# One-core linear attention and mixture of experts: 64-token transposes, keyed state first, deeper load buffers, routing one step at a time, zeros after the attention

## Chip, cores and metric

The kernel runs on one core of a Trainium2 chip. The metric is the device time of one execution in microseconds (us). The kernel before took 589.33 us, the median of three runs (588.52, 589.33 and 590.4).

## What is computed

A linear attention with a decaying state (4 batches, 8 heads, 768 tokens, 48 features a head), whose output, seen as 3072 tokens of 384 features, goes into a mixture of 8 experts with noisy top-2 routing. Everything is float32.

```python
for t in range(S):                                   # S = 768
    cur = einsum('bhd,bhe->bhde', u * k[t], v[t])
    y[:, :, t] = einsum('bhd,bhde->bhe', r[t], state + cur)
    state = w[:, :, None] * state + einsum('bhd,bhe->bhde', k[t], v[t])
x = y.transpose(0, 2, 1, 3).reshape(3072, 384)
noisy = x @ w_gate + log1p(exp(x @ w_noise)) * noise
top2 = the two largest of noisy, top2_w = their softmax
for e in range(8):
    out[mask] += top2_w * (relu(x[mask] @ w1[e]) @ w2[e])   # 384 -> 1024 -> 384
```

## The kernel before, in words

The kernel has two stages. The **attention** goes over 24 blocks of 128 tokens: iteration i takes chunk i // 4 of batch i % 4, so that chunk 0 (iterations 0 to 3) has no state yet and chunk 5 (20 to 23) leaves none. The **experts** follow, expert 0 in three pieces of its tokens, the others in two; each piece is a first layer (`p1`, L984) and a second (`p2`, L1018), and the result is scattered to `out`.

The order on each engine is the order of the program text (`manual_schedule`); each engine takes its own instructions strictly in that order, and semaphores tie them together. One iteration of the attention is made of:

- loads of k, r and v for block i + 3 (`load`, L139, issued from SyncE, which also writes x and loads weights in the same queue). Four buffers each (`NLD`).
- on GpSimd, `prep_k(i + 2)` (keys by powers of the decay, L349) and `uterm_a(i + 2)` (the u term, L356 and L360), two instructions for each product, and the scaling of the state (L430).
- on TensorE, `trans(i + 1)`: four transposes of 128x128 for k, four for r (L387); `xtrans(i - 1)`: three for the finished x (L475); `kvup` (L417, 16 matmuls for the state); `yout` (L448, 32 matmuls of the masked scores and, from chunk 1, 16 of the state); `logits(i - 1)` (L489, 12 matmuls); `scores(i + 1)` (L399, 16 matmuls of 64 rows, two of which share the array).
- on VectorE, the copy of r out of PSUM with its weights (`rT`, L392), the sum of the u term (`c`, L368), for i up to 8 its product with v (`cv`, L377; after that on ScalarE, L380), the output `x` (L465), the state sum (`zt`, L429), and the two masks of the scores (`am`, L407).
- on ScalarE, the copies of k (L390) and x (L477) out of PSUM, the state's block form (`zblock`, L437), the logits (L491).

Into this order the program lays the **routing**. `route(g)` is a generator of some 55 small VectorE steps for a group of 8 blocks (64 columns wide at most); `rstep(us)` takes as many steps from it as a credit in microseconds allows, in three places of an iteration (0.6, 0.85 and 0.2 us). Most steps read what the step just ahead of them wrote. Routing of blocks 0 to 7 runs from iteration 8, that of 8 to 15 after it, that of 16 to 23 in expert 0. Weights of expert 0 are split into a high and a low part: one ScalarE copy (L313), one VectorE difference (L318) for each of seven pieces (`W_LD`, `W_HI`, `W_LO`). In iteration 21 (`I_EARLY`) the first two tiles of expert 0 are gathered by GpSimd DMAs (`xgather`, L903) and in iteration 22 transposed (`xT`, L926). From iteration 16 on `zero_out` writes half of the zeros that `out` starts from (8 of 16 DMAs), the rest follow in the first layer of expert 0.

Of the kernel before, what the change touches and what calls it, by code (L numbers as in the profile page):

```python
# [31 lines left out]
STEPS_A = 0.6  # L32
STEPS_B = 0.85
STEPS_KV = 0.2
# [5 lines left out]
NLD = 4  # L40
XT_AT = 4
# [5 lines left out]
W_LD = {1: (0,), 3: (1,), 4: (2,), 5: (3,), 6: (4,), 7: (5,), 8: (6,)}  # L47
W_HI = {4: (0,), 5: (1,), 6: (2,), 7: (3,), 8: (4,), 21: (5,), 22: (6,)}
W_LO = {4: (0,), 5: (1,), 6: (2,), 7: (3,), 8: (4,), 22: (5,)}
# [3 lines left out]
def kernel(  # L53
# [44 lines left out]
    psum = ctx.enter_context(tc.tile_pool(name="psum", bufs=1, space=bass.MemoryType.PSUM))  # L98
    dram = ctx.enter_context(tc.tile_pool(name="dram", bufs=1, space=bass.MemoryType.DRAM))
# [7 lines left out]
    att_pool = [att]  # L107

# [18 lines left out]
    rd = [att.tile([128, H, 64], F32, name=f"rd{j}", bufs=1) for j in range(NLD)]  # L127
    rt, kt, vt = {}, {}, {}

    def load(i, part=(0, 3)):  # L130
        c, b = divmod(i, B)
        for nm, src, dst in (("kt", k, kt), ("rt", r, rt), ("vt", v, vt))[part[0]:part[1]]:
            if nm == "rt":
                t = rd[i % NLD][:, :, :D]
            elif i or nm == "vt":
                t = att.tile([128, H, D], F32, name=nm, bufs=NLD)
# [23 lines left out]
    pwarm = psum.tile([128, 512], F32, name="pwarm", tag="kv")  # L160

    def warm(n):
# [4 lines left out]
    warm(WARM0)  # L167
# [14 lines left out]
    mneg = const.tile([128, 1, 128], I32, name="mneg")  # L182
# [17 lines left out]
    kT, rT = {}, {}  # L200

    def turn0(src, dst, pw, nm):
        pt = psum.tile([128, NP, 128], F32, name="pt0", tag="pa", bufs=2)
        for p in range(NP):
            nc.tensor.transpose(pt[:, p, :], src[:, 2 * p:2 * p + 2, :].rearrange("p a b -> p (a b)"), ident)
        t = att.tile([128, NP, 128], F32, name=nm, bufs=1 if nm == "kT" else 2)
        nc.vector.tensor_mul(t, pt, pw)
        dst[0] = t

    tabk = att.tile([128, H, 64], F32, name="tabk", bufs=1)  # L210
    turn0(kd[0], kT, pwk, "kT")
    ptab = psum.tile([128, NP, 128], F32, name="ptab", tag="pt", bufs=2)
# [3 lines left out]
    turn0(rd[0], rT, pwr, "rT")  # L216
# [7 lines left out]
    nc.vector.tensor_mul(w128, tmpw[:, :, 63:64], tmpw[:, :, 63:64])  # L224
# [4 lines left out]
    kvp = pwarm[:, :NP * D].rearrange("p (a d) -> p a d", d=D)  # L229
# [24 lines left out]
    zrow = att.tile([128, DM], F32, name="zrow", bufs=1)  # L254

    def consts_a():
        nc.vector.tensor_scalar(ltri, idif, 0.0, None, op0=ALU.is_gt)
        nc.gpsimd.memset(ones_b, 1.0)
        nc.gpsimd.memset(acc, 0.0)
        for t in ZB:  # L260
            nc.gpsimd.memset(t, 0.0)
# [3 lines left out]
        nc.vector.tensor_copy(ieu, ie)  # L265
        nc.vector.tensor_scalar(ie_n[:, 0, :], ie, float(LS), None, op0=ALU.mult)
# [7 lines left out]
        nc.gpsimd.iota(thi, pattern=[[1, NT], [0, 2]], base=1, channel_multiplier=0, **imp)  # L274

# [21 lines left out]
    def w_split(e):  # L297
# [3 lines left out]
        def unit(mat, c0, c1, src):  # L301
            def f():
# [7 lines left out]
                nc.sync.dma_start(tv, src)  # L310
                for _ in range(NLAG[0]):
                    yield
# [28 lines left out]
    AM, X, CV, PY, PA = {}, {}, {}, {}, {}  # L341

# [23 lines left out]
    def uterm_b(i):  # L366
        c8 = att.tile([128, H, 1], F32, name="c8")
        nc.vector.tensor_reduce(c8, RKU[i], AX.X, ALU.add)  # L368
        C8[i] = c8
        if i <= GROUPS[0][1]:  # L370
            uterm_c(i)

    def uterm_c(i):
        c8 = C8[i]
        cv = att.tile([128, H, D], F32, name="cv")
        if i <= GROUPS[0][1]:
            nc.vector.tensor_mul(cv, vt[i], c8.to_broadcast([128, H, D]))  # L377
        else:
            for h in range(H):
                nc.scalar.activation(cv[:, h, :], vt[i][:, h, :], AF.Copy, scale=c8[:, h, :])  # L380
        CV[i] = cv

    def trans(i):
        for src, store, nm in ((kd[i % 3], kT, "kT"), (rd[i % NLD], rT, "rT")):
            pt = psum.tile([128, NP, 128], F32, name="pt", tag="pt", bufs=2)
            for p in range(NP):
                nc.tensor.transpose(pt[:, p, :], src[:, 2 * p:2 * p + 2, :].rearrange("p a b -> p (a b)"), ident)  # L387
            t = att.tile([128, NP, 128], F32, name=nm, bufs=1 if nm == "kT" else 2)
            if nm == "kT":
                nc.scalar.activation(t, pt, AF.Copy)  # L390
            else:
                nc.vector.tensor_mul(t, pt, pwr)  # L392
            store[i] = t

    def scores(i):
        pa = [psum.tile([128, NP, 128], F32, name="pa", tag="pa", bufs=2) for _ in range(2)]
        for p in range(NP):
            for s in range(2):
                nc.tensor.matmul(pa[s][:, p, :], kT[i][s * 64:(s + 1) * 64, p, :],  # L399
# [3 lines left out]
    def mask(i):  # L403
        pa = PA[i]
        am = att.tile([128, 2, NP, 128], F32, name="am", bufs=1)
        for s in range(2):
            nc.vector.tensor_tensor(am[:, s].bitcast(I32), pa[s].bitcast(I32),  # L407
                                    mneg.to_broadcast([128, NP, 128]), op=ALU.bitwise_and)
# [11 lines left out]
    def zup(i):  # L420
# [3 lines left out]
        if c == 0:  # L424
            for p in range(NP):
                nc.scalar.activation(Z[b][:, p, :], kvp[:, p, :], AF.Copy, scale=w128[:, p, :])
        else:
            src = att.tile([128, NP, D], F32, name="zt", bufs=1)
# [1010 lines left out]
```

## Time and profile before

| | us |
|---|---|
| median of the runs | 589.33 |
| profiled execution | 590.02 |
| its span, first to last instruction | 588.3 |
| attention, first `py` matmul to the last x | 11.1 to 129.6 |
| busy TensorE, VectorE, ScalarE, GpSimd | 575.7, 359.2, 286.1, 276.9 |

In the profile a busy time is the time in which an engine works on at least one instruction. Matmuls are pipelined, so that their starts, not their durations, tell how fast they follow each other; the same holds for VectorE, where an instruction's duration can reach into the next one's. DMA is the mean busy share of 16 DMA engines.

### The profile page before, as it was taken

To read this page: it belongs to the slowest core of one execution; us is meant where nothing else is said; L and a number is where in the kernel's file an instruction comes from. 1 tells how busy PE (TensorE), PEld (TensorE's weight loads), DVE (VectorE), ACT (ScalarE), POOL (GpSimd) and SP (SyncE) were. 2 spreads that over 40 slices of the span, in tenths; PEclk is the share of its full clock that TensorE was granted. 3 is DMA by queue.
4 is the path that set the end of the run, shared out by engine and by line. 5 is a ranking of instruction groups with operands and counts; after the bars stand their busy time and mean duration, and the time that the engine had idled before them with its cause. 6 is when DMAs were issued, how large, how long until landed. Compare 5 with 4: busy or idle time off the path is not lost.

```text
span 588.3 us, 13208 instructions
## 1 busy us (share of the span) xinstructions
PE 575.7 (98%) x5011; PEld 547.6 (93%) x5012; DVE 359.2 (61%) x855; ACT 286.1 (49%) x726; POOL 276.9 (47%) x422
## 2 busy tenths in 40 slices
PE   8999999989999999999999999999999999999995
PEld 5888898979999999999999999999999999999995
DVE  7899998988875734556454554546355546454331
ACT  3656677752363624455445544454544455445220
POOL 8989876811016543336344442534253446423222
PEclk9999999999999999999999999999999999999998
DMA  9999988946315645655565646464745546423211
GB/s 149 215 227 221 208 178 194 219 129 174 111 35 174 212 123 130 186 125 173 111 183 133 176 122 189 104 184 136 165 128 142 171 124 193 119 81 85 67 36 42
DMA packets 143015, 86.42 MB, mean 147 GB/s; under 512 B 118415, under 2 KB 133006, under 8 KB 142944
## 3 DMA queue, kind: packets, MB, share of 16 engines
q1 hardware_dynamic: 132384, 56.67, 40.0%
q0 software_dynamic: 9936, 28.83, 15.8%
q8 instruction: 41, 0.67, 0.5%
q14 instruction: 30, 0.25, 0.1%
q10 hardware_dynamic: 624, 0.00, 0.1%
HBM read 58.83 MB, written 19.76 MB: 134 GB/s over the span
## 4 chain that ended last, share of the span: by engine, by line
PE 87%; DMA 5%; DVE 4%; POOL 2%; issue 1%; ACT 0%; SPq 0%; POOLq 0%; DVEq 0%
PE ph L984 37%; PE pym L1018 34%; PE py L448 3%; DMA kt<-in_k_dram 2%; PE pa L399 2%; PE pym L1011 2%; PE pym L1009 2%; PE pt L387 2%; DMA stg<-in_moe_w_dram 1%; DMA xg<-xd,GR 1%; DVE am L407 1%; PE pwarm L417 1%; PE pl L489 1%; PE ptm L926 1%; PE ptx L475 1%
## 5 line engine op out<-in xcount | busy, mean ns | idle before, releaser
L1018 PE MATMUL pym<-w1h,hb 128*128 128x384 f32 x768 | 200.8, 338 | 0.0
L988 DVE SCALAR_TENSOR_TENSOR hb<-ph,hb 128x384 fp32r<-128x384 f32 (+1 forms) x136 | 72.3, 533 | 111.8 <-ACT ht L986 61.1
L1018 PEld LDWEIGHTS pym<-w1h,hb 128*128 128x128 f32 x768 | 139.6, 188 | 0.3
L984 PE MATMUL ph<-xh,w0h 128*128 128x384 f32 (+3 forms) x408 | 139.8, 343 | 0.0
L984 PE MATMUL ph<-xh,w0l 128*128 128x384 f32 (+3 forms) x408 | 138.8, 341 | 0.0
L984 PE MATMUL ph<-xl,w0h 128*128 128x384 f32 (+3 forms) x408 | 133.6, 341 | 0.0
L1018 PE MATMUL pym<-w1l,hb 128*128 128x384 f32 x384 | 129.8, 338 | 0.0
L986 ACT ACTIVATE hb<-ph 128x384 fp32r<-128x384 f32 (+1 forms) x136 | 64.3, 473 | 107.0 <-PE ph L984 103.8
L1041 POOL DMA_INDIRECT out_dram<-ot,TK x56 | 59.2, 1058 | 98.5 <-DVE ot L1037 45.9
L903 POOL DMA_INDIRECT xg<-xd,GR x56 | 59.4, 1061 | 69.6 <-DVE GR L768 20.4
L984 PEld LDWEIGHTS ph<-xh,w0h 128*128 128x128 f32 x408 | 76.7, 188 | 3.1
L984 PEld LDWEIGHTS ph<-xh,w0l 128*128 128x128 f32 x408 | 76.7, 188 | 2.6
L984 PEld LDWEIGHTS ph<-xl,w0h 128*128 128x128 f32 x408 | 76.1, 188 | 2.7
L912 POOL DMA_INDIRECT pv<-out_dram,GA x49 | 51.9, 1059 | 47.9 <-DMA out_dram<-ot,TK 35.5
L1018 PEld LDWEIGHTS pym<-w1l,hb 128*128 128x128 f32 x384 | 72.1, 188 | 0.1
L959 ACT ACTIVATE xh<-xj 128x384 fp32r<-128x384 f32 (+1 forms) x42 | 21.1, 502 | 43.7 <-DVE xj L957 38.3
L1026 ACT ACTIVATE ot<-pym 128x384 f32<-128x384 f32 x39 | 18.9, 485 | 39.3 <-PE pym L1018 24.0
L448 PE MATMUL py<-vt,am 128*64 128x48 f32 x768 | 36.8, 219 | 0.7 <-DVE am L407 0.7
L960 DVE TENSOR_TENSOR xl<-xj,xh 128x384 fp32r<-128x384 f32 (+1 forms) x42 | 22.3, 532 | 24.7 <-ACT xh L959 17.5
L945 ACT ACTIVATE pl<-xg 128x768 uint16<-128x768 uint16 (+1 forms) x42 | 35.3, 841 | 0.9 <-DMA xd<-pl 0.9
L318 DVE TENSOR_TENSOR w0l<-stg,w0h 128x1024 fp32r<-128x1024 f32 x24 | 29.4, 1241 | 6.8 <-ACT w0h L313 6.8
L448 PEld LDWEIGHTS py<-vt,am 128*64 128x64 f32 x768 | 32.1, 137 | 1.4 <-DVE am L407 1.0
(255 smaller groups left out, 862.3 us busy)
## 6 DMA issues: line engine op xcount, KB each, us to landing
stg<-in_moe_w_dram SPq DMA_DIRECT2D x24, 512.0 KB
stg<-in_moe_w_dram SPq DMA_DIRECT2D x32, 384.0 KB
rd<-in_r_dram SPq DMA_DIRECT2D x24, 192.0 KB
vt<-in_v_dram SPq DMA_DIRECT2D x24, 192.0 KB
xd<-x SPq DMA_DIRECT2D x24, 192.0 KB
out_dram<-zrow SPq DMA_DIRECT2D x16, 288.0 KB
kt<-in_k_dram SPq DMA_DIRECT2D x23, 192.0 KB
xg<-xd,GR POOLq DMA_INDIRECT x56
```

What stands on the lines that cost most here:

```text
L318: nc.vector.tensor_sub(lo, tv, hi.bitcast(F32))
L448: nc.tensor.matmul(o[qs], lhsT[:, qs], rhs, start=first[q], stop=last, skip_group_check=True)
L903: nc.gpsimd.indirect_dma_start(out=xg[:n], out_offset=None, in_=xd[:rows_of(early_)], in_offset=bass.IndirectOffsetOnAxis(ap=GR[:n, e * NJ ...
L912: nc.gpsimd.indirect_dma_start(out=pv[:n], out_offset=None, in_=out, in_offset=bass.IndirectOffsetOnAxis(ap=GA[:n, e * NJ + t:e * NJ + t + ...
L945: nc.scalar.activation(pl[:n], XG[e, t][:n, :DM].bitcast(U16).rearrange("p (d two) -> p two d", two=2), AF.Copy)
L959: nc.scalar.activation(xh, xj, AF.Copy)
L960: nc.vector.tensor_sub(xl, xj, xh.bitcast(F32))
L984: nc.tensor.matmul(ph[:, :w_], a[:, d, fs], x[:, d, :w_], start=(j == 0), stop=(j == len(q) - 1))
L986: nc.scalar.activation(h_[:, f, 0, :], ph[:, a:b], AF.Relu)
L988: nc.vector.scalar_tensor_tensor(h_[:, f, 1, :], ph[:, a:b], 0.0, h_[:, f, 0, :].bitcast(F32), op0=ALU.max, op1=ALU.subtract)
L1018: nc.tensor.matmul(py, hb[:, f, a, hs], x[:, f, :], start=(j == 0), stop=(j == len(q) - 1))
L1041: st = nc.gpsimd.indirect_dma_start(out=out, out_offset=bass.IndirectOffsetOnAxis(ap=TK[:n, q:q + 1], axis=0), in_=ot[:n], in_offset=None, ...
```

## The change

- **Transposes.** k, r and x are transposed in halves of 64 tokens: each 128x128 transpose becomes two with 64 rows of input and 64 columns of output, on the two row halves of the array, written to two PSUM banks (`KX` for k and x, `RV` for r and the state, `PAB` for the scores).
- **Order.** An iteration begins with `kvup` and `yout`, whose state part comes first and which takes the logits of the block before (in the same PSUM bank); then come the transposes of k and r for block i + 2, the scores of i + 1 and the transposes of the x just made. GpSimd's u term is made for i + 1, its state scaling one iteration later. The state of chunk 0 is scaled on VectorE in one instruction, not on ScalarE in four.
- **Loads.** Six buffers for k, r and v; k and r are loaded 6 blocks ahead, v 5. The room comes from the expert activations `hb` and `ht`, which now lie where the attention's tiles were.
- **Routing.** `one_step()` takes one step; there are eight calls in an iteration: two after the state sum, two after the sum of the u term, one each after x, after `rT`, between the two masks and at the end.
- **Expert weights.** The split of each of the seven pieces is cut into two halves, one in each iteration from `W_AT0`; the loads are spread to iteration 14.
- **Zeros.** All 16 DMAs come in the first layer of expert 0. The x tiles of expert 0's first piece are transposed in iteration 23.
- Some constants move: the zeros of the state blocks from GpSimd to ScalarE, three small VectorE ones behind iteration 0.

```diff
-    def trans(i):
-        for src, store, nm in ((kd[i % 3], kT, "kT"), (rd[i % NLD], rT, "rT")):
-            pt = psum.tile([128, NP, 128], F32, name="pt", tag="pt", bufs=2)
-            for p in range(NP):
-                nc.tensor.transpose(pt[:, p, :], src[:, 2 * p:2 * p + 2, :].rearrange("p a b -> p (a b)"), ident)
...
+    def turn_rows(dst, o, src, base=0):
+        for s in range(2):
+            q = slice(base + s * 64, base + (s + 1) * 64)
+            nc.tensor.transpose(dst[:, s, o:o + 64], src[q], ident[q, q])
...
+    def turn_kr(i):
+        if i >= NT:
+            return
+        for src, dst in ((kd[i % 3], KX), (rd[i % NK], RV)):
             for p in range(NP):
+                turn_rows(dst, p * 64, pair(src, p))
+        kT[i] = att.tile([128, NP, 128], F32, name="kT", bufs=2)
+        nc.scalar.activation(by_row(kT[i]), halves_of(KX, 0, NP), AF.Copy)
+        rT[i] = att.tile([128, NP, 128], F32, name="rT", bufs=2)
+        nc.vector.tensor_mul(by_row(rT[i]), halves_of(RV, 0, NP), by_row(pwr))
+        one_step()
...
+        for h in (slice(0, NP // 2), slice(NP // 2, NP)):
+            nc.vector.tensor_tensor(am[:, :, h].bitcast(I32), pa[:, :, h].bitcast(I32),
+                                    mneg[:, None].to_broadcast([128, 2, NP // 2, 128]), op=ALU.bitwise_and)
+            if h.start == 0:
+                one_step()
...
+    def one_step():
+        k = 0
+        while len(route_q) > k and not at_pe[0]:
+            try:
+                c = next(route_q[k])
...
+            if c == "pe":
+                at_pe[0] = 2
+            return
...
     for i in range(NT):
-        if i + NLD - 1 < NT and i + NLD - 1 > 2:
-            load(i + NLD - 1)
-        if i >= NT - 8:
-            zero_out(i - NT + 8)
-        if i + 1 < NT:
-            trans(i + 1)
...
+        products(i)
+        if i + 6 < NT:
+            load(i + 6, (0, 2))
...
+        if i:
+            kvup(i)
         yout(i)
-        xout(i)
...
+        if i + 5 < NT:
+            load(i + 5, (2, 3))
+        zup_v(i)
         if i:
             zblock(i - 1)
-        rstep(STEPS_B)
...
+            uterm_c(i, CV_EARLY, H)
+            logits_out(i - 1)
+            route_when_done(i - 1)
+        tick()
+        one_step()
+        one_step()
+        if i + 1 < NT:
+            uterm_b(i + 1)
+        one_step()
+        one_step()
+        xout(i)
+        one_step()
         if i == NT - 1:
+            xT_first()
+            turn_x(i)
             p1a = p1(0, 0)
+        else:
+            turn_kr(i + 2)
+            uterm_c(i + 1, 0, CV_EARLY)
             scores(i + 1)
+            turn_x(i)
             mask(i + 1)
+            tick()
+            one_step()
...
     for j, _ in enumerate(p1a):
-        zero_out(8 + j)
+        zero_out(2 * j)
+        zero_out(2 * j + 1)
         rstep(STEPS_P1)
+    zero_out(14)
     zero_out(15)
```

## Rows read from the trace of the kernel before

**Rows 1.** Busy time by stage: span, engines with counts, TensorE clock, DMA share, GB/s.

```profile
11.10:49.60 38.50, 37.52 (x755) 33.31 (x751) 35.90 (x63) 21.27 (x57) 34.78 (x56) 1.00 0.97 212
49.60:97.20 47.60, 47.30 (x1004) 43.23 (x1000) 43.90 (x123) 34.62 (x120) 39.52 (x71) 1.00 0.91 200
97.20:129.60 32.40, 29.91 (x579) 26.67 (x574) 28.64 (x90) 22.83 (x80) 17.79 (x31) 1.00 0.72 180
129.60:588.30 458.70, 452.23 (x2630) 439.15 (x2630) 243.36 (x560) 203.24 (x462) 175.30 (x227) 1.00 0.47 134
```

**Rows 2.** The chain that ended last: start us, length us, what.

```profile
57.35 5.32 DMA kt<-in_k_dram
...
120.24 6.07 DMA xg<-xd,GR
...
126.35 0.55 PE ptm L926 x3
...
129.00 0.56 DVE x L465
...
130.22 1.06 PE ph L984 x9
```

**Rows 3.** TensorE's timeline, one iteration: start us, us, engine, line, operation, shape, count.

```profile
70.03 0.56 PE L417 MATMUL pwarm<-vt,kd 128*48 128x48 f32 x16
...
72.20 0.53 PE L489 MATMUL pl<-wg,xT 128*64 128x64 f32 x12
72.67 1.16 PE L399 MATMUL pa<-rT,kT 64*128 64x128 f32 x16
73.76 0.66 PE L387 MATMUL pt<-ident,kd 128*128 128x128 f32 x4
...
74.69 0.49 PE L475 MATMUL ptx<-ident,x 128*128 128x128 f32 x3
75.11 0.39 PE L417 MATMUL pwarm<-vt,kd 128*48 128x48 f32 x8
```

**Rows 4.** Weight loads by line, 65 to 97 us: count, busy us, mean ns, idle.

```profile
L399 PEld LDWEIGHTS pa<-rT,kT 64*128 64x128 f32 x96 | 5.8, 187 | 0.4
...
L489 PEld LDWEIGHTS pl<-wg,xT 128*64 128x64 f32 x78 | 2.9, 138 | 0.0
L387 PEld LDWEIGHTS pt<-ident,rd 128*128 128x128 f32 x24 | 2.8, 141 | 0.0
```

**Rows 5.** VectorE's timeline, where routing steps meet other work.

```profile
58.29 0.21 DVE L512 SCALAR_TENSOR_TENSOR r1r<-RT,r1r 128x64 f32<-128x64 f32 x1
58.54 0.23 DVE L514 TENSOR_SCALAR RT<-r1r 128x64 f32<-128x64 f32 x1
58.81 0.23 DVE L517 SCALAR_TENSOR_TENSOR RT<-RT,r1r 128x64 f32<-128x64 f32 x1
58.95 0.35 DVE L429 TENSOR_TENSOR zt<-pwarm,z 128x192 f32<-128x192 f32 x1
59.21 1.28 DVE L407 TENSOR_TENSOR am<-pa,mneg 128x512 int32<-128x512 int32 x2
60.41 0.22 DVE L517 SCALAR_TENSOR_TENSOR RT<-RT,r1r 128x64 f32<-128x64 f32 x1
60.54 0.68 DVE L392 TENSOR_TENSOR rT<-pt,pwr 128x512 f32<-128x512 f32 x1
```

**Rows 6.** VectorE's groups by line, 11 to 130 us: busy, mean ns, idle before, releasers.

```profile
L407 DVE TENSOR_TENSOR am<-pa,mneg 128x512 int32<-128x512 int32 x46 | 29.4, 680 | 1.9 <-PE pa L399 1.7
...
L465 DVE TENSOR_TENSOR x<-py,cv 128x384 f32<-128x384 f32 x24 | 13.2, 552 | 2.6 <-PE py L448 1.4 <-ACT r_ob L604 0.9
L368 DVE TENSOR_REDUCE c<-rku 128x8 f32<-128x384 f32 x24 | 13.0, 542 | 1.4 <-POOL rku L360 1.4
...
L318 DVE TENSOR_TENSOR w1l<-stg,w1h 128x768 fp32r<-128x768 f32 x3 | 3.1, 1047 | 0.0
...
L928 DVE TENSOR_TENSOR xl<-ptm,xh 128x384 fp32r<-128x384 f32 x2 | 1.1, 558 | 1.2 <-ACT xh L927 1.2
```

More of the change, by code (lines that the diff above doesn't have):

```diff
@@ L40 @@
 NLD = 4
+NV = 6
+NK = 6
 XT_AT = 4
@@ L126 @@
     kd = [att.tile([128, H, 64], F32, name=f"kd{j}", bufs=1) for j in range(3)]
-    rd = [att.tile([128, H, 64], F32, name=f"rd{j}", bufs=1) for j in range(NLD)]
+    rd = [att.tile([128, H, 64], F32, name=f"rd{j}", bufs=1) for j in range(NK)]
     rt, kt, vt = {}, {}, {}
@@ L449, in acc_mm @@
             first[q] = False
+        for p in range(NP if c else 0):
+            for q in range(2):
+                acc_mm(py[:, 2 * p:2 * p + 2, :], rT[i][:, p, :], ZB[b][:, p, :], q, False)
+        if i:
+            logits(i - 1, not c)
         for p in range(NP):
-            if c:
-                for q in range(2):
-                    acc_mm(py[:, 2 * p:2 * p + 2, :], rT[i][:, p, :], ZB[b][:, p, :], q, False)
             for s in range(2):
@@ L467, in xout, with logits, logits_out @@
         nc.sync.dma_start(xd[i * 128:(i + 1) * 128, :DM], x)
-    LG = {}
-    XT = {}
-    def xtrans(i):
-        pt = psum.tile([128, ND, 128], F32, name="ptx", tag="py1")
+    def logits(i, alone):
         for d in range(ND):
-            nc.tensor.transpose(pt[:, d, :], X[i][:, d * 128:(d + 1) * 128], ident)
-        t = att_pool[0].tile([128, ND, 128], F32, name="xT", bufs=1)
-        nc.scalar.activation(t, pt, AF.Copy)
-        XT[i] = t
-    def logits(i):
+            for q in range(2):
+                qs = slice(q * 64, (q + 1) * 64)
+                nc.tensor.matmul(PL[i][qs], XT[i][:, d, qs], wg[:, d, None, :].to_broadcast([128, LREP, 2 * E]),
+                                 start=alone and d == 0, stop=(d == ND - 1), skip_group_check=True)
+    def logits_out(i):
         g = [i >= a for a, _ in GROUPS].count(True) - 1
@@ L1050, with tick @@
     hold = []
+    load(3)
     wun = w_split(0)
+    route_q = []
+    at_pe = [0]
+    credit = [0.0]
+    def tick():
+        for x in late_mm:
+            x[0] -= 1
+            if x[0] == 1:
+                x[2]()
+        while late_mm and late_mm[0][0] <= 0:
+            late_mm.pop(0)[1]()
+            credit[0] -= 0.25
+        at_pe[0] = max(at_pe[0] - 1, 0)
+    def one_step():
[3 more added lines that the diff above has]
+                c = next(route_q[k])
+            except StopIteration:
+                route_q.pop(k)
+                continue
+            if c == "wait" and k == 0 and FILL:
+                k = 1
+                continue
+            if c == "pe":
+                at_pe[0] = 2
+            return
     consts_a()
@@ L1060 @@
     mask(0)
+    load(4)
+    load(5, (0, 2))
     warm(WARM3)
-    route_q = []
-    at_pe = [0]
-    credit = [0.0]
+    turn_kr(1)
+    uterm_b(0)
+    nc.vector.tensor_mul(w128, tmpw[:, :, 63:64], tmpw[:, :, 63:64])
     def rstep(us, lag=2):
@@ L1246 @@
         wstep()
-    att_pool[0] = late[0]
     step, xt = stepper(STEPS_R, 0, 2, (4, 5, 6))
@@ L1386 @@
                 nc.sync.dma_start(X[i], xd[i * 128:(i + 1) * 128, :DM])
-                xtrans(i)
-                logits(i)
+                pt = psm[0].tile([128, ND, 128], F32, name="s_pt", tag="pt", bufs=2)
+                for d in range(ND):
+                    nc.tensor.transpose(pt[:, d, :], X[i][:, d * 128:(d + 1) * 128], ident)
+                XT[i] = slow.tile([128, ND, 128], F32, name="xT", bufs=1)
+                nc.vector.tensor_copy(XT[i], pt)
+                pl_alone(i)
                 for g in range(len(GROUPS)):
```

249 lines of the change are left out of this document (134 added, 115 removed).

## The prediction

> **What bounds the kernel now.** I read the busy times by stage first. In the last stretch, the experts from 129.6 us on, TensorE is busy 452.2 of 458.7 us [rows 1]; what it does there is not touched, so a gain must come from the attention ahead of it, and it reaches the end in full, as the first matmul of the experts (130.22) follows the last x (129.00) at once [rows 2]. In the attention, 11.1 to 129.6 us, two engines are nearly full: TensorE 37.5 + 47.3 + 29.9 = 114.7 and VectorE 35.9 + 43.9 + 28.6 = 108.4 of 118.5 us [rows 1]. Relief for one of them alone therefore gives only what the other leaves. The chain runs mostly over TensorE, with two intrusions by DMAs: arrivals of k (one of 5.32 us) around 48 to 63 us, and the gather that ends at 126.3 and holds up TensorE for the tiles of expert 0 [rows 2]. One undisturbed iteration takes 75.11 - 70.03 = 5.08 us [rows 3].
>
> **Transposes, on TensorE.** By the starts in [rows 3], k and r take 74.69 - 73.76 = 0.93 us for eight transposes, x 0.42 for three with the change to the next shape; together 1.35. They become 22 halves, eleven pairs that can share the array as the scores do. No row shows such a pair. One bound is the pair of logits (72.67 - 72.20 = 0.47 for six pairs, 0.08 each: 64 columns loaded, 64 streamed), the other the pair of scores (1.09 for eight, 0.136 each: 128 loaded, 128 streamed) [rows 3]. Which is nearer is told by the weight loads: a 128-column load of a transpose lasts 141 ns, like the 64-column load of the logits with 138, while the 128-column load of the scores lasts 187 [rows 4]. I take 0.08: 0.86 us an iteration, 0.49 less than now; with 0.136 it is 1.50, 0.15 more. TensorE's iteration then needs 4.6 us (5.2 at the other end). Matmuls for state, outputs, logits and scores are the same in number; only their order differs.
>
> The Trainium skill speaks against this part: "TensorE: Matmul & The Clock Gate", section LDWEIGHTS, has the time of a load depend on its columns and not on its rows, and half a transpose still loads 128 columns. By that rule nothing is saved. The loads of 141 and 187 ns for the same 128 columns [rows 4] show that columns alone don't set it.
>
> **VectorE, what is added and taken away.** Up to the last x:
> - The seventh weight piece is split inside the attention, not behind it: +1.05 [rows 6].
> - The state of chunk 0 moves here from ScalarE, four instructions like `zt`, which takes 59.21 - 58.95 = 0.26 [rows 5]: +1.05.
> - Three constants come after iteration 0: at most 0.25 each by the step rows [rows 5]: +0.75.
> - More routing. The calls in the code: group 0 has 55 steps and starts at the end of iteration 8; one matmul pause in 13 costs it that iteration; it ends in 16. Group 1 starts in 17, pauses in 21 and reaches step 48 by the last x. Before, it stood at about 41 there. Seven more of 0.14: +1.0.
> - The two `xl` of expert 0's first tiles come after the last x: -1.1 [rows 6].
> - Steps one by one. A step followed by the step that reads it takes 0.25 to 0.27 us to the next start (58.29, 58.54, 58.81); followed by other work it takes 0.13 to 0.14 (58.81 to 58.95, 60.41 to 60.54) [rows 5]. So 0.11 are saved for each step that gets other work behind it, 0.08 of them busy time and 0.03 gap. Of VectorE's 63 + 123 + 90 = 276 instructions in the attention [rows 1], 155 are the work of the blocks, weights and constants, and 121 routing; I count 84 of these with routing right behind. After, six of eight calls have other work behind them, so of some 125 routing instructions about 48 are followed by another: 36 fewer. Busy -2.9, gaps -1.1.
>
> Busy sum: 108.4 + 1.05 + 1.05 + 0.75 + 1.0 - 1.1 - 2.9 = 108.2 us. Its idle time now is 118.5 - 108.4 = 10.1: waits for the scores 1.9, for `yout` and others before x 2.6, for the u term 1.4, before `xl` 1.2 [rows 6], and some 3.0 in the gaps of 0.03 between dependent steps. After, gaps 1.9, u term 1.4; the wait before `xl` falls behind the last x; the waits for scores and `yout` (4.5) go where TensorE needs 4.6 us against VectorE's (108.2 / 23.3 iterations) 4.65 and more once routing runs; I leave 1.5 of them for the first iterations. Idle 4.8. VectorE thus needs 108.2 + 4.8 = 113.0 instead of 118.5: **-5.4 us**. What is late next is VectorE itself.
>
> The Trainium skill has a rule against the steps one by one as well: "VectorE: DVE Perf Modes", section The DRAIN you can't avoid, lets no instruction start until the one before it has left the pipeline, whatever it reads, though it adds that one which is not held starts earlier. By its first half this part is worth nothing, the rival "no cheaper" below. The trace differs: 0.13 against 0.25 [rows 5].
>
> **The rest.** GpSimd has the same products; in the first eight iterations it is busy 34.8 of 38.5 us [rows 1], so that these can't shrink below 35, which is also VectorE's need there (35.9, less two weight pieces that come later, plus state and constants: about 35). ScalarE loses the 16 scalings, gains the zeros of the state blocks: far from full (21.3 of 38.5, 34.6 of 47.6). Loads: 72 of 192 KB, 24 writes of x and seven weight pieces are about 22 MB; at the 212 GB/s of the first stretch 104 us from the start, so all is there before 124; the deeper buffers keep this queue full and end the waits for k. The zeros leave the attention (2.4 MB) and meet the second piece's gather: 4.7 MB issued within some 9 us need 23 us at 200 GB/s, and that gather, 6 us long in a busier time [rows 2], is wanted some 15 us after the last x. Its price is 0 to 4 us; I take 0.4. The first gather is issued in iteration 21 as before but used one iteration later, which ends its wait. Waits that are new: `yout` of i + 1 can't start before x and the logits have left their shared bank; x is one instruction ahead of r's copy and the masks on VectorE, over 2 us before TensorE wants it, so nothing queues behind it. Zero for that, 0.5 either way for the start.
>
> **Sum.** -5.4 + 0.4 = -5.0. The span of 588.3 becomes 583.3 and the profiled execution 590.02 becomes 585.0; as it lies 0.7 above the median of the runs, I predict **584.3 us**.
>
> **Rivals.**
> 1. *A pair of halves is as dear as a pair of scores* (0.136). TensorE stays at 5.1 to 5.2 us an iteration and remains the bound; the waits for k and for the first gather (about 1.5) still go: 587.8. For: 128 columns are loaded. Against: the 141 ns [rows 4].
> 2. *Steps one by one are no cheaper.* 4.0 of the gain are gone: 588.3. For: the steps that hold two instructions keep their inner dependence. Against: [rows 5].
> 3. *Slower: the halves don't share the array and each costs what a whole transpose costs*, 0.93 / 8 = 0.116 us. Then 22 x 0.116 = 2.55 against 1.35, 1.2 more in each of 24 iterations, less the 1.5 of waits: about +27, 616 us. It decides from about 0.11 us a pair, where TensorE's iteration passes VectorE's. Against: the scores' pairs share it at 0.136 for two matmuls of 128 columns [rows 3].
> 4. *Rival 2 and the full 4 us of the second gather behind the zeros*: 592.3.
> 5. *Better: no wait is left* (-3 more on VectorE): 581.
>
> **How the numbers follow.** Chances: forecast 0.54 (581.5 to 587.5, by its idle time of 2 to 7 us), better 0.06, rival 1 0.12, rival 2 0.12, rival 3 0.07, rival 4 0.09. About 0.3% (1.8 us) is what a measurement of this kernel can tell from no change. Faster: 0.54 + 0.06 = 0.60; the same: 0.12 + 0.12 = 0.24; slower: 0.07 + 0.09 = 0.16. The range leaves out rival 3 and the far tails: 580 to 592.5; both signs are in it, but the forecast's own range is 581.5 to 587.5.
>
> **What the profile after would show.** Starts of transposes about 0.08 us apart for a pair, and TensorE with idle time in the attention (right), or no idle time and pairs at 0.11 or more (rivals 1 and 3). VectorE over 95% busy from iteration 8 on, routing steps with 0.14 to the next start. No wait of `kd` for k. The last x at about 124 us, and TensorE full from there on; a wait of the transposes of expert 0's second piece for their gather would be rival 4. The forecast is wrong if the attention ends at 124 and the time doesn't follow, or if VectorE's base work (masks 29.4, x 13.2 us [rows 6]) gets longer in the new shapes.

## The result, and the profile after

| | before | after |
|---|---|---|
| median of the runs, us | 589.33 | 594.2 |
| span of the profiled execution | 588.3 | 592.5 |
| last x starts | 129.0 | 132.3 |
| from there to the end of the span | 459.3 | 460.2 |

The change makes the kernel slower: ratio 1.0076, interval 1.0052 to 1.0099; forecast were 584.3 us and a range of 580 to 592.5. Of the 4.2 us between the two profiled executions 3.3 lie in the attention and 0.9 behind it.

The busy time by stage, columns as in [rows 1], for the kernel after:

```profile
11.10:49.60 38.50, 35.08 (x867) 32.63 (x862) 35.17 (x71) 17.63 (x43) 34.49 (x58) 0.96 0.90 184
49.60:97.20 47.60, 39.85 (x993) 37.08 (x991) 44.65 (x124) 34.57 (x116) 36.78 (x64) 0.96 0.98 217
97.20:132.90 35.70, 29.04 (x706) 26.29 (x700) 30.63 (x101) 24.55 (x87) 19.55 (x33) 1.00 0.44 104
132.90:592.50 459.60, 452.80 (x2633) 438.74 (x2633) 242.51 (x554) 203.94 (x465) 174.08 (x227) 1.00 0.50 138
```

Up to the end of the last x, TensorE is busy 35.08 + 39.85 + 29.04 = 104.0 us, 10.7 fewer than in [rows 1]: the relief came. VectorE is busy 110.5 of 121.8 us, where it was 108.4 of 118.5: 2.0 more, and its idle time, which should have halved, went from 10.1 to 11.3.

TensorE's timeline of one iteration (start us, us, engine, line, operation, shape, count) shows the halves:

```profile
75.56 0.85 PE L499 MATMUL py<-zb,rT 128*64 128x96 f32 x16
...
77.61 0.47 PE L217 MATMUL KX<-ident,kd 64*128 64x64 f32 x8
77.91 0.41 PE L217 MATMUL RV<-ident,rd 64*128 64x64 f32 x8
78.16 1.11 PE L443 MATMUL PAB<-rT,kT 64*128 64x128 f32 x16
79.11 0.35 PE L217 MATMUL KX<-ident,x 64*128 64x64 f32 x6
...
79.95 0.85 PE L499 MATMUL py<-zb,rT 128*64 128x96 f32 x16
```

Four pairs for r take 78.16 - 77.91 = 0.25 us, 0.0625 a pair; those for k 0.30. For k and r together 0.55 where [rows 3] have 0.93.

By the starts of x, the profiled executions differ like this:

| x | before | after | difference gained or lost in this stretch |
|---|---|---|---|
| 0 | 12.9 | 15.2 | +2.3 |
| 8 | 51.5 | 50.5 | -3.3 |
| 10 | 62.3 | 63.5 | +2.2 |
| 17 | 97.2 | 102.3 | +3.9 |
| 22 | 122.7 | 128.9 | +1.1 |
| 23 | 129.0 | 132.3 | -2.9 |

The start is later and made up by x 8. Around x 8 to 10 the chain of waits after has two loads of weights for which ScalarE stood 4.6 us; from 133.33 on it runs over TensorE:

```profile
39.24 5.69 DMA stg<-in_moe_w_dram
...
50.63 4.86 DMA stg<-in_moe_w_dram
...
133.33 1.33 PE ph L1044 x9
```

Between x 16 and x 17 stands a wait that the kernel before doesn't have. VectorE's timeline after (the bracket is idle time and its releaser):

```profile
97.93 0.34 DVE L476 TENSOR_TENSOR zt<-RV,z 128x192 f32<-128x192 f32 x1
99.71 0.17 DVE L660 COPY L<-RT 128x14 f32<-128x14 f32 x1 [1.43 <-PE RT L656]
...
102.28 0.55 DVE L518 TENSOR_TENSOR x<-py,cv 128x384 f32<-128x384 f32 x1
```

VectorE waits 1.43 us for a matmul of the routing (L656) that stands behind the outputs in TensorE's line, and x with it. Two like waits stand before `acc` (group rows below: 2.8 us).

TensorE's own idle time up to the last x is 121.8 - 104.0 = 17.8 us, where it was 3.8. Most of it stands at one place: before the transposes of the x just made, which the new order puts ahead of the next block's state and outputs. Three of these waits in TensorE's timeline after:

```profile
58.84 0.58 PE L217 MATMUL KX<-ident,x 64*128 64x64 f32 x6 [2.87 <-DVE r1r L556]
...
96.36 0.40 PE L217 MATMUL KX<-ident,x 64*128 64x64 f32 x6 [1.34 <-DVE x L518]
...
102.98 0.40 PE L217 MATMUL KX<-ident,x 64*128 64x64 f32 x6 [1.28 <-DVE RT L551]
```

In all there are 13 such waits, 12.8 us; twelve of them end 0.06 to 0.15 us behind the end of x. The kernel before transposes x one iteration later, and up to the last x TensorE never stands for it. The chain that ended last shows what the order ties together: the transposes of x, its copy, its logits, and behind them in the same line the outputs of the next block, which the next x needs.

```profile
123.66 1.37 PE KX L217 x6
125.11 0.50 ACT xT L437
125.66 0.57 PE py L527 x12
126.23 0.92 PE py L499 x32
```

### The profile page after: what moved, and what is told of

It is laid out like the page before. It is cut to its first block, busy times and chain, and to the rows that moved or that the text cites. A ratio compares the mean times of both kernels' runs of the same rounds, so it can differ in the third digit from the quotient of the medians.

```text
span 592.5 us, 13758 instructions
## 1 busy us (share of the span) xinstructions
PE 565.8 (96%) x5281; PEld 540.4 (91%) x5282; DVE 359.4 (61%) x866; ACT 286.5 (48%) x721; POOL 274.0 (46%) x420
## 4 chain that ended last, share of the span: by engine, by line
PE 79%; DVE 10%; DMA 5%; ACT 2%; POOL 2%; issue 2%; POOLq 0%; SPq 0%; ACTq 0%
PE ph L1044 35%; PE pym L1078 33%; PE py L499 2%; PE pym L1069 2%; PE pym L1071 2%; DVE am L451 2%; DMA stg<-in_moe_w_dram 2%; DVE x L518 2%; DVE rT L430 1%; DMA xg<-xd,GR 1%; DMA out_dram<-ot,TK 1%; PE KX L217 1%; DVE c L410 1%; PE py L527 1%; PE PAB L443 1%
## 5 line engine op out<-in xcount | busy, mean ns | idle before, releaser
L947 POOL DMA_INDIRECT xg<-xd,GR x56 | 61.2, 1092 | 70.6 <-DVE r_oa L636 18.8
L956 POOL DMA_INDIRECT pv<-out_dram,GA x49 | 49.8, 1016 | 48.2 <-DMA out_dram<-ot,TK 35.8
L391 POOL TENSOR_TENSOR kd<-kt,tabk 128x192 f32<-128x192 f32 x46 | 27.7, 624 | 12.8 <-PE RV L463 6.4
L451 DVE TENSOR_TENSOR am<-PAB,mneg 128x512 int32<-128x512 int32 x48 | 31.6, 680 | 1.9 <-PE PAB L443 1.8
L419 ACT ACTIVATE cv<-vt,c 128x48 f32<-128x48 f32 x120 | 30.2, 323 | 5.0 <-DVE c L410 2.6
```

The lines of the kernel that those rows point to most:

```text
L391: nc.gpsimd.tensor_mul(KD[i][:, h], kt[i][:, h], tabk[:, h, :D])
L419: nc.scalar.activation(CV[i][:, h, :], vt[i][:, h, :], AF.Copy, scale=C8[i][:, h, :])
L451: nc.vector.tensor_tensor(am[:, :, h].bitcast(I32), pa[:, :, h].bitcast(I32), mneg[:, None].to_broadcast([128, 2, NP // 2, 128]), op=ALU.b ...
L947: nc.gpsimd.indirect_dma_start(out=xg[:n], out_offset=None, in_=xd[:rows_of(early_)], in_offset=bass.IndirectOffsetOnAxis(ap=GR[:n, e * NJ ...
L956: nc.gpsimd.indirect_dma_start(out=pv[:n], out_offset=None, in_=out, in_offset=bass.IndirectOffsetOnAxis(ap=GA[:n, e * NJ + t:e * NJ + t + ...
```

## Experiments

Ratios are to the kernel before, run beside them on the same chip; the changed kernel stands at 1.0076 by the same measure.

### Does TensorE's work set the pace?

**Every half transposed twice** (changed kernel):

```diff
             nc.tensor.transpose(dst[:, s, o:o + 64], src[q], ident[q, q])
+        for s in range(2):
+            q = slice(base + s * 64, base + (s + 1) * 64)
+            nc.tensor.transpose(dst[:, s, o:o + 64], src[q], ident[q, q])
```

> The changed kernel with every half transpose done twice. Eleven pairs more in an iteration, at the 0.062 us between the starts of two pairs in its trace: 0.68 us of TensorE work more in each of 24 iterations. Theory V (VectorE sets the pace of the attention, TensorE has slack): at most 1.5 us longer. Theory T (TensorE, by its work or because it waits in line for x ahead of the state and output matmuls, sets the pace): up to 15 us longer.

Measured: 597.61 us, 1.0129 (1.0110 to 1.0148). Its busy row up to the last x:

```profile
11.10:138.30 127.20, 116.68 (x3084) 110.04 (x3080) 112.33 (x295) 76.59 (x244) 91.64 (x155) 1.00 0.76 167
```

TensorE has 12.7 us more, the ratio rises by 0.0053, some 3.1 us: a quarter gets through, more than theory V allows and far less than theory T's bound.

**k and x whole again** (changed kernel; r stays in halves):

```diff
-                turn_rows(dst, p * 64, pair(src, p))
+                if dst is KX:
+                    nc.tensor.transpose(KX[:, 0, p * 128:(p + 1) * 128], pair(src, p), ident)
+                else:
+                    turn_rows(dst, p * 64, pair(src, p))
...
-            turn_rows(KX, XO + d * 64, X[i][:, d * 128:(d + 1) * 128])
+            nc.tensor.transpose(KX[:, 1, d * 128:(d + 1) * 128], X[i][:, d * 128:(d + 1) * 128], ident)
```

> The changed kernel with one part undone: from iteration 1 on, k and x are transposed whole, k into one bank of PSUM and x into the other, instead of as halves that share both banks; r stays in halves. TensorE gets about 0.4 us more to do in an iteration, as seven whole ones at .116 stand for seven pairs at .062. Theory V (TensorE has room, VectorE sets the pace): between no change and 1.5 us slower, 594 to 596. Theory T (what the prediction rested on, that relief of TensorE shortens the iteration): 4 us slower or more, 598. Theory S (the shared banks make TensorE wait for ScalarE's copy of k, 8 us of waits in the changed kernel, and this costs more than the halves save): 1.5 to 4 us faster, 590 to 592.5.

Measured: 1.0063 (1.0039 to 1.0087; 595.45 us beside 591.11 for the kernel before), no different from the changed kernel.

```profile
11.10:134.50 123.40, 112.78 (x2396) 99.09 (x2394) 110.76 (x294) 76.94 (x245) 90.87 (x155) 0.99 0.80 171
```

8.8 us of TensorE's relief given back cost nothing at the end. The edit also ends the sharing of two banks by k and x, which theory S prices, and TensorE's waits for x fall from 12.8 to 7.2 us; a gain by that could hide a loss by the longer transposes, and no run parts the two. The clock doesn't decide either: in the changed kernel, with TensorE idle 3.4 and 7.8 us in the first two stages, it was granted at 0.96 there, a mean of time at 2.4 and at 1.2 GHz (it was low around 18 and 60 us, near TensorE's waits of 1.49 and 2.87 us for x); here it is 0.99, with every half done twice 1.00, and neither of the two is faster.

**Halves alone in the kernel before** (k and r in halves in one tile `KR` of two banks, x whole):

```diff
+                for s in range(2):
+                    q = slice(s * 64, (s + 1) * 64)
+                    nc.tensor.transpose(KR[:, s, o + p * 64:o + p * 64 + 64],
+                                        src[q, 2 * p:2 * p + 2, :].rearrange("p a b -> p (a b)"), ident[q, q])
```

> The kernel before, with one part of the change alone: k and r are transposed as 64-token halves into two banks of PSUM, x stays whole, all else is as it was. In the changed kernel a pair of halves took .062 us against .141 for one whole, so eight pairs save some .6 us of TensorE in an iteration of 5.08. Theory T (TensorE's line sets the pace of the kernel before, as the prediction had it): twelve to sixteen iterations at up to .4 us, 3 to 5 us faster, 584 to 587. Rival V (VectorE's line is full in the same iterations and takes over at once): less than 1.5 us faster, 588 to 590.

The 0.141 us of this expectation is the length of a weight load [rows 4]; whole transposes start 0.116 us apart [rows 3], so that some 0.4 us an iteration were to be saved, not 0.6. Measured: 620.51 us, 1.0508 (1.0482 to 1.0534). Neither theory: the longest wait (us in total, times, longest) is a new one,

```profile
PEld KR L394 <- ACT kT L399: 39.3, 23, 2.7
```

the halves of r stand behind ScalarE's copy of k out of the same tile. With all sixteen halves ahead of both copies:

```diff
                     nc.tensor.transpose(KR[:, s, o + p * 64:o + p * 64 + 64],
...
+        for o, src, store, nm in both:
             half = KR[:, :, o:o + 256].rearrange("p s (a t) -> p s a t", t=64)
```

> The kernel before, with k and r transposed as 64-token halves as in the run before this one, but all sixteen halves issued ahead of the two copies out of PSUM. In the run before, the halves of r stood behind ScalarE's copy of k out of the same PSUM tile, 39 us in all, so that it measured this wait and not the halves. Theory T (TensorE's line sets the pace of the kernel before, as the prediction had it): 3 to 5 us faster, 584 to 587. Rival V (VectorE's line, full as well, takes over at once): less than 1.5 us faster, 588 to 590. If the one tile for k and r still makes TensorE wait for copies, slower than 590, with that wait in the rows.

Measured: 593.26 us, 1.0048 (1.0023 to 1.0073), slower than before.

```profile
11.10:131.50 120.40, 109.13 (x2489) 97.23 (x2485) 107.96 (x274) 77.84 (x257) 90.94 (x156) 1.00 0.87 195
```

```profile
PEld py L459 <- DVE am L418: 4.6, 11, 0.9
DVE rT L403 <- ACT kT L401: 4.5, 7, 0.9
```

TensorE's busy time falls from 114.7 to 109.1 us and the attention gets 1.9 longer. TensorE now waits for masks, and the copy of r behind that of k. The second wait comes with this edit, which has one tile for k and r where the kernel before has two. So less work for TensorE, busy 97% of the attention in the kernel before, became idle time here; what the halves would do without the shared tile is not shown.

### Does VectorE's work set it?

**The state sum made twice** (one more VectorE instruction an iteration):

```diff
             nc.vector.tensor_add(ZT[i], kvp, Z[b])
+            nc.vector.tensor_add(ZT[i], kvp, Z[b])
```

> The changed kernel with the state sum zt made twice: one VectorE instruction of 0.27 us more in each of the 16 iterations 4 to 19. Theory V: nearly all of 16 x 0.27 = 4.3 us show at the end. Theory T: under 1 us, since VectorE would have room.

Measured: 596.37 us, 1.0118 (1.0089 to 1.0147).

```profile
11.10:135.10 124.00, 104.74 (x2548) 95.56 (x2543) 115.28 (x310) 77.18 (x245) 90.70 (x155) 0.99 0.77 171
```

4.8 us more busy time, 2.5 us at the end: between the two theories.

**Weight pieces split whole**, not in halves (changed kernel):

```diff
-                    nc.scalar.activation(part[0][1], part[0][0], AF.Copy)
+                    nc.scalar.activation(hi, tv, AF.Copy)
...
-                    nc.vector.tensor_sub(part[0][2], part[0][0], part[0][1].bitcast(F32))
+                    nc.vector.tensor_sub(lo, tv, hi.bitcast(F32))
```

> The changed kernel, with each weight piece split by one copy on ScalarE and one difference on VectorE, instead of two half copies and two half differences. Fourteen half differences of some .65 us each hold VectorE 9.7 us up to the last x in the changed kernel; seven whole ones at the 1.16 us of the kernel before hold it 8.1. Theory V (VectorE's time is what sets the end of the attention): 1.6 us of busy time go and the time falls by 1 to 1.7 us, to 592.5 to 593.2. Rival: the differences wait for longer copies on ScalarE and nothing is gained, 594.

Measured: 593.45 us, 1.0064 (1.0043 to 1.0085), 0.7 us less with the intervals overlapping.

```profile
11.10:133.00 121.90, 104.69 (x2550) 96.67 (x2547) 107.78 (x287) 76.56 (x238) 91.08 (x154) 0.97 0.79 174
```

VectorE's busy time falls by 2.7 us, its idle time rises by 2.8, and the last x comes when it came. In time this is between theory V and its rival.

**Eight routing steps in two bunches of four** (changed kernel), behind the state sum and at the end of the iteration:

```diff
-        one_step()
-        one_step()
+        for _ in range(4):
+            one_step()
```

> The changed kernel, with the eight routing steps of an iteration given in two bunches of four rather than one by one. Theory A (separating the steps saves what the prediction took, a dependent step .25 us and a separated one .13): six separated steps become dependent in each of some fifteen iterations, 90 x .115 = 10 us more on VectorE's line, of which 5 to 8 show at the end, 599 to 602. Rival B (what separation saves is given back, since a step between attention steps waits for GpSimd or TensorE as often as for the step before it): within 1.5 us of the changed kernel, 593 to 596.

Measured: 595.61 us, 1.0102 (1.0077 to 1.0128): 1.5 us slower, the rival's range. The interval overlaps with the changed kernel's, so that a gain by steps one by one is not shown.

```profile
11.10:134.20 123.10, 105.50 (x2550) 97.77 (x2545) 112.79 (x295) 77.07 (x245) 88.39 (x154) 0.96 0.78 172
```

VectorE is busy 2.3 us more, where theory A had 10.

### Single parts: start, loads of weights, zeros

The u term's sum behind x in iterations 0 and 1 (changed kernel):

```diff
-        if i + 1 < NT:
+        if 1 < i < NT - 1:
             uterm_b(i + 1)
...
+        if i < 2:
+            uterm_b(i + 1)
```

> The changed kernel with the sum of the u term of blocks 1 and 2 put behind the masks, as the kernel before has it. In the trace of the changed kernel x of block 0 stands behind that sum on VectorE, which waits for GpSimd until 14.15 us, and comes at 15.2 instead of 12.9. If this start is a loss that stays: 2 to 2.5 us shorter. Rival: GpSimd gives the pace of the first iterations anyway, x of block 0 comes earlier and x of block 8 does not: no change (within 0.7 us).

Measured: 1.0087 (1.0069 to 1.0105). x 0 starts at 13.0 as before, x 8 at 51.0 against 50.5: what the start loses isn't on the path to x 8. The rival holds.

Earlier loads of the weights (changed kernel):

```diff
-W_LD = {1: 0, 3: 1, 5: 2, 7: 3, 9: 4, 11: 5, 14: 6}
-W_AT0 = (4, 6, 8, 11, 13, 16, 18)
+W_LD = {0: 0, 1: 1, 2: 2, 7: 3, 8: 4, 9: 5, 13: 6}
+W_AT0 = (4, 5, 6, 10, 11, 12, 16)
```

> The changed kernel with the loads of expert 0's first three weight pieces in iterations 0, 1, 2 (now 1, 3, 5) and their splits from iterations 4, 5, 6 (now 4, 6, 8), the others from 10, 11, 12 and 16. Theory Q (the deep buffers put the weights behind ten microseconds of queued loads; ScalarE waits for them in line, and with it the products that x needs, around iteration 9): the wait of 4.6 us of ScalarE for weights goes and the attention ends 2 to 3 us earlier. Rival: VectorE makes up for that stall, since its work is the same in sum: no change.

Measured: 1.0086 (1.0066 to 1.0106), the rival. ScalarE's wait of 4.6 us for weights is gone and the loss moves: x 8 at 53.7 against 50.5, x 10 at 63.6 against 63.5.

The zeros moved alone (kernel before):

```diff
-        if i >= NT - 8:
-            zero_out(i - NT + 8)
...
-        zero_out(8 + j)
+        zero_out(2 * j)
+        zero_out(2 * j + 1)
```

> The kernel before, with one part of the change alone: all sixteen pieces of zeros are written behind the last x, two with each step of the first expert piece, and none in iterations 16 to 23. In the kernel before a gather of 6.07 us ends at 126.3 and TensorE stands for it ahead of the last x; in the changed kernel the step from x 22 to x 23 is 2.9 us shorter. Theory Z (the zeros in the queue make this gather long): 1.5 to 3 us faster, 586 to 588. Rival 1 (the gather is as long without them): no change, 589 to 590. Rival 2 (the zeros, now behind the attention, delay the gathers of the second piece): slower than before, 590 to 593.

Measured: 589.17 us, 0.9995 (0.9980 to 1.0011). In its profiled execution the last x comes 1.6 us earlier and the span is 586.7, but the timed runs don't show it: rival 1.

### The order of the routing

**Routing matmuls ahead of the outputs** in TensorE's line (changed kernel):

```diff
-        late_mm.append([2, lambda: place(n, oa, ob, wp_, w_, c0, first),
+        late_mm.append([3 if in_att else 2, lambda: place(n, oa, ob, wp_, w_, c0, first),
...
-                at_pe[0] = 2
+                at_pe[0] = 1
```

> The changed kernel, with the routing matmuls put ahead of the output matmuls in TensorE's line again, at the first of the two places instead of behind them. In the changed kernel VectorE stood 1.43 us at 99.7, .61 us at 82.4 and 2.24 us at 127.5 for a routing matmul that stood behind outputs. Theory W (part of the loss is this wait, as every routing step now stands between attention steps on one engine): these three waits go, some 4 us of VectorE's idle time, and the time falls by 2.5 to 4 us, to 590 to 592. Rival V (VectorE's idle time only changes places, since a chunk's chain must pass all engines anyway): less than 1 us.

Measured: 594.18 us, 1.0067 (1.0046 to 1.0088), by its time rival V: no different from the changed kernel. The wait for the matmul is gone, and x waits 1.00 us for ScalarE instead; the same place in VectorE's timeline:

```profile
97.08 0.34 DVE L476 TENSOR_TENSOR zt<-RV,z 128x192 f32<-128x192 f32 x1
97.34 0.54 DVE L410 TENSOR_REDUCE c<-rku 128x8 f32<-128x384 f32 x1
98.87 0.56 DVE L518 TENSOR_TENSOR x<-py,cv 128x384 f32<-128x384 f32 x1 [1.00 <-ACT lg L536]
```

The last x starts at 129.6, 2.7 us earlier, and the span is 593.4, 0.9 longer. TensorE's waits for gathers up to 230 us, in the changed kernel and here (us in total, times, longest):

```profile
PE ptm L970 <- DMA xg<-xd,GR: 0.2, 1, 0.2
...
PE ptm L971 <- DMA xg<-xd,GR: 2.1, 3, 1.1
```

The tiles of expert 0's second piece wait for their gather. Its rows come from the routing of blocks 8 to 15, whose last steps stand between the activations of the first piece on VectorE, and with the edit six fewer of its instructions stand ahead of the last x (120 against 126). Three runs on that, all on top of this edit:

**Six more calls of routing directly behind the last x:**

```diff
+    for _ in range(6):
+        rstep(STEPS_P1)
     for j, _ in enumerate(p1a):
```

> The changed kernel with the routing matmuls ahead of the outputs, which ended the attention 2.7 us earlier (last x done at 130.2 instead of 132.9) and lost 3.3 us of it again, as TensorE waited for the gathers of expert 0's second piece, whose rows come from routing steps that stand between the activations of the first piece on VectorE. Here six more calls of routing follow directly behind the last x, some 18 steps earlier in VectorE's line. Theory G (the gathers, set by the routing steps, are what is late next): the waits of the transposes for the gathers go and 2.5 to 4 us come back, 590 to 592. Rival (the activations that now stand behind these steps hold up TensorE's first piece by as much): 593 to 595.

Measured: 597.30 us, 1.0135 (1.0108 to 1.0163), the opposite. The last x starts at 127.7; then TensorE's own line stands for the routing's matmuls:

```profile
132.12 0.17 PE L688 MATMUL RT<-acc,ones_b 128*128 128x8 bf16 x1 [1.54 <-DVE GTS L786]
...
134.92 0.35 PE L657 MATMUL RT<-r_ob,r_oa 128*128 128x16 bf16 x8 [1.47 <-DVE PS L694]
```

**A fourth step for three between two activations** so that expert matmuls stay in between:

```diff
         zero_out(2 * j + 1)
-        rstep(STEPS_P1)
+        rstep(1.0)
```

> The changed kernel with the routing matmuls ahead of the outputs in the attention (as in the run that ended the attention 2.7 us earlier and waited 3.3 us for gathers behind it), and here with a fourth routing step for three between two activations of expert 0's first piece, so that expert matmuls still stand between the routing matmuls on TensorE. Theory G (the gathers of the second piece, whose rows come from the routing's chain, are what is late next): the chain of some eighteen steps is through about 2 us sooner, the waits for these gathers shrink and the time falls to 591.5 to 593. Rival (VectorE is the bound there too and the activations get late): 594 to 596.

Measured: 591.72 us beside 591.11 for the kernel before, 1.0012 (0.9987 to 1.0037), theory G's range; and once more, unchanged, beside the last run below:

> The run with one more step for an activation once more, unchanged, on the same chip as the run beside it, so that the two can be compared: 0 to 1.5 us over the kernel before by either theory.

590.93 us, 1.0008 (0.9984 to 1.0033). The wait for the gathers fell to

```profile
PE ptm L971 <- DMA xg<-xd,GR: 1.0, 2, 0.8
```

Both measurements agree: level with the kernel before. The fourth step without the moved matmuls was not run, in the changed kernel or in the kernel before. In the two profiled executions of this one kernel the last x starts at 130.0 and 132.0, which says how far a single one may be trusted.

**The second piece's rows taken as known**, its gathers directly behind the last x:

```diff
-        xgather(0, g, g)
+        if not g:
+            xgather(0, g, g)
...
     pl_alone(NT - 1)
+    xgather(0, 1, 0, 2)
...
```

> The changed kernel with the routing matmuls ahead of the outputs in the attention, and with the gathers of expert 0's second piece taking the rows of its first piece, which are known in iteration 21 (so the second piece computes on the wrong tokens); they are issued directly behind the last x. Theory G (only the routing's chain makes these gathers late): TensorE has no wait for them at 146 to 150, the 2 us lost there come back, and with the third piece's waits left the time is 591 to 592.5. Rival (the gathers are late by the queue they stand in, or TensorE then waits elsewhere): 593.5 to 595.

Measured: 1.0058 (1.0034 to 1.0081). The waits around 148 us are gone, as theory G has it, but the third piece's gathers are now late, so that by the experts' fourth piece 2.9 us are lost there against the kernel before; in this execution the last x started at 132.3. Its time, 595.37 us, is just past the rival's range.

**Together, with whole weight splits** and more steps in the next two stages too:

```diff
-STEPS_P1 = 0.8
-STEPS_P2 = 4.2
+STEPS_P1 = 1.0
+STEPS_P2 = 5.2
```

> What helped so far, together: the changed kernel with the routing matmuls ahead of the outputs in the attention, a fourth routing step for three between the activations of expert 0's first and second piece, a quarter more between the outputs of the first, and whole weight splits. The run with the first two of these ended the attention at 130.5 and still waited 0.8 us for the gathers of the third piece. Theory G (the routing's chain behind the attention is what was late): these waits go too, and the time is 0 to 2 us under that of the kernel before. Rival V (steps moved forward load VectorE where the activations stand): as the run before it, 0 to 1.5 us over the kernel before.

Measured: 592.67 us, 1.0035 (1.0016 to 1.0053), neither theory. The last x starts at 127.1, earlier than in any other kernel, and by the starts of the experts' pieces 3.7 us are lost behind it against the kernel before; TensorE waits for activations and routing again:

```profile
PE ph L1040 <- DVE ht L1044: 1.0, 1, 1.0
PE RT L652 <- ACT r_ob L643: 0.9, 1, 0.9
```

## Why the prediction was wrong, point by point

**Transposes, right.** Taken 0.08 us a pair, measured 0.0625 to 0.075; undisturbed, TensorE's iteration is 79.95 - 75.56 = 4.39 us by the starts of two successive state parts of `yout`, taken 4.6. Rivals 1 and 3 fall. Loads of halves take 141 ns (group rows below), as loads of whole blocks did [rows 4]. Between these two the trace agrees with the Trainium skill, "TensorE: Matmul & The Clock Gate", section LDWEIGHTS, by which the rows of a load don't matter. That nothing is saved does not follow from it: pairs start 0.0625 us apart, so that the loads overlap.

**"VectorE thus needs 108.2 + 4.8", the step that failed.** I took idle time as what is left when the other engine is full, so that relief of TensorE would take it away. Measured are 110.5 us busy and 11.3 idle, 121.8 for 113.0: of the 8.8 us too many 2.3 are busy time and 6.5 the idle time that stayed. VectorE's and TensorE's groups after, 11 to 132.9 us, as in [rows 6] and [rows 4]:

```profile
L451 DVE TENSOR_TENSOR am<-PAB,mneg 128x512 int32<-128x512 int32 x46 | 30.3, 680 | 0.9 <-PE PAB L443 0.8
...
L518 DVE TENSOR_TENSOR x<-py,cv 128x384 f32<-128x384 f32 x24 | 13.2, 549 | 2.7 <-ACT lg L536 2.7
...
L349 DVE TENSOR_TENSOR w1l<-stg,w1h 128x384 fp32r<-128x384 f32 x4 | 2.5, 634 | 0.0
L346 DVE TENSOR_TENSOR w1l<-stg,w1h 128x384 fp32r<-128x384 f32 x4 | 2.5, 626 | 0.0
...
L561 DVE SCALAR_TENSOR_TENSOR RT<-RT,r1r 128x64 f32<-128x64 f32 x10 | 2.3, 226 | 0.1
...
L709 DVE TENSOR_TENSOR r_s<-r_s 128x64 f32<-128x64 f32 x2 | 1.0, 511 | 0.0
...
L767 DVE TENSOR_TENSOR acc<-acc,r_sm 128x8 bf16<-128x8 bf16 x2 | 0.8, 392 | 2.8 <-PE RT L766 2.8
```

```profile
L217 PEld LDWEIGHTS KX<-ident,kd 64*128 64x128 f32 x176 | 7.4, 141 | 1.7 <-issue 0.4
```

The wait of the masks for the scores went down as forecast (1.9 to 0.9). That of x stayed (2.6, now 2.7) with ScalarE as its releaser, and 2.8 before `acc` and 1.4 before `L` are new. One engine's work taken away (10.7 us on TensorE, 2.7 on VectorE in the run with whole splits) turned into idle time, and work added got through by a quarter (TensorE) or a half (VectorE). I read this as a round through four engines, each with a fixed order, in which each step waits for some other engine; which link of the round sets the pace no run shows. GpSimd's waits for k, which the deeper buffers were to end, fell only from 6.4 to 5.2 us.

**Terms of VectorE's busy time.** Each instruction is counted to its end or to the next start, whichever comes first: state of chunk 0 1.16 (taken 1.05), constants 1.12 (0.75), `xl` -1.03 (-1.1). Mis-sized were two. The weights took 9.19 us against 6.96, +2.2 for the +1.05 taken: I overlooked that two halves of 626 and 634 ns are more than one whole of 1047 [rows 6]. And the routing, 126 instructions in 24.07 us against 119 in 23.63: +0.4 where +1.0 and -2.9 were taken. The separation came nearly as counted (steps with routing right behind them fell from 82 to 54, taken 84 to 48), and its price was right (0.131 us to the next start), but other steps got longer, as the last section shows. A constant that I didn't count (`w128`) took 0.55, and the rest of VectorE's work got 2.3 us shorter. By the bunches the separation is worth some 1.5 us at the end, and that is not clear of noise: rival 2, "no cheaper", may be right in the time.

**"Nothing queues behind it. Zero for that", failed too.** I looked for waits behind `yout` and found none. Two were there. TensorE stands 12.8 us for x ahead of its transposes, with the next `yout` in line behind them; what that costs at the end is not shown, as no run puts these transposes back by one block. And the routing's matmuls behind `yout` I left out, though I had counted their pauses as iterations without steps. Moving them alone gave 1.0067, no clear gain; moved and with a fourth step for three behind the last x the kernel is level with the one before. The two together are worth 1.0076 - 1.0010 = 0.0066, 3.9 us of the 4.5. How much of it is the wait and how much the faster routing in the experts, which could help the kernel before as well, is not shown.

**"A gain reaches the end in full", failed.** Last x at 129.6, 127.7 and 127.1 gave 1.0067, 1.0135 and 1.0035. Behind the last x stands the chain of the routing, then a gather, then TensorE; a faster attention meets it. The waits of rival 4, for the second gather, are 0.2 us in the changed kernel; with the routing's matmuls moved they came (2.1 us), by this chain: with its rows taken as known those around 148 us were gone. That rival 4's time, 592.3, is the nearest of those worked out is luck. It also counts 0.4 us twice (591.9 without), and idle times of 2 to 7 us would give 581.5 to 586.5, not 587.5.

**Start and zeros.** x 0 is 2.3 us later, outside the 0.5 either way, but the run with the sum behind x shows that this costs nothing. The first gather's wait did end: the step from x 22 to x 23 is 2.9 us shorter. The zeros moved alone are worth nothing that the timed runs show.

Open stays which part of the 3.9 us between x 10 and x 17 is the routing's longer steps and which TensorE's waits for x: no run took either away.

## What to carry to other kernels

When two engines are nearly full, don't add up one engine's busy time and a smaller idle time: take work from each in turn on the chip first, and see whether the end moves. Before pricing relief of a stage, look for the chain that runs beside it into the next one (here routing, rows, gather), since the gain ends where that chain becomes late. An order of small steps that is moved drags its matmuls past other matmuls: look where they stand in TensorE's line, and whether work that needs a block's result now stands ahead of work that doesn't.

## What the runs showed of the hardware

VectorE steps that read two SBUF operands wait for GpSimd. The timelines of VectorE and of GpSimd after:

```profile
111.24 0.21 DVE L707 TENSOR_TENSOR r_s<-RT,r_d 128x64 f32<-128x64 f32 x1
111.48 0.57 DVE L709 TENSOR_TENSOR r_s<-r_s 128x64 f32<-128x64 f32 x1
111.97 0.63 DVE L710 SCALAR_TENSOR_TENSOR r_sn<-r_s,nz 128x64 f32<-128x64 f32 x1
112.52 0.54 DVE L410 TENSOR_REDUCE c<-rku 128x8 f32<-128x384 f32 x1
...
146.92 0.23 DVE L709 TENSOR_TENSOR r_s<-r_s 128x64 f32<-128x64 f32 x1
```

```profile
111.46 0.51 POOL L480 TENSOR_TENSOR z<-zt,w 128x192 f32<-128x192 f32 x1 [1.06 <-DVE r_s L707]
111.93 1.14 POOL L398 TENSOR_TENSOR rku<-rd,kt 128x192 f32<-128x192 f32 x2
```

The step of L709 takes 0.57 us and ends 0.08 behind the GpSimd product of 111.46 to 111.97; the same step at 146.92, with GpSimd idle, takes 0.23. Steps that read the routing's PSUM tile (L561, 226 ns) stay as they were. In the attention fifteen routing steps with two SBUF inputs took 0.30 us or more (0.30 to 0.70); fourteen of them end 0.02 to 0.15 us behind a GpSimd product, and the fifteenth is sixteen times as wide (128x1024). The Trainium skill has this in "SBUF — State Buffer", section "SBUF: two separate sides": a VectorE instruction with two SBUF inputs and a GpSimd instruction that reads SBUF hold a shared port in turn, each for its whole length. The trace agrees in these rows, and the rule, had I weighed it, spoke against scattering such steps over the iteration.
